# The first x tile as two transfers, and a query product ahead of the second tile's transposes

## The chip, the cores and the metric

The kernel runs on one core of a Trainium2 chip. The core has five engines that run side by side and synchronise by semaphores: PE (TensorE, matrix products; its weight loads are shown apart as PEld), DVE (VectorE), ACT (ScalarE), POOL (GpSimd) and SP (SyncE, here used to issue DMA transfers). ACT and POOL issue DMA transfers too. The metric is the device time of one execution in microseconds, the median of several executions.

## The reference

A gated mix of two branches over x, which has 2048 tokens of 640 features, in bf16. Cut to what matters:

```
x = A_x                                            # 1 x 2048 x 640
g = sigmoid((x * gate_w).sum(-1))
# branch A: linear attention, 32 heads of 20
q, k, v = split(x @ wqkv)
phi(t) = where(t > 0, t + 1, exp(t)) + 1e-6
o = (phi(q) @ (phi(k).T @ v)) / (phi(q) . sum(phi(k)) + 1e-6)      # per head
a = o @ wo
# branch B: token-shift mixer and MLP
h  = gelu(layernorm(x) @ w1);  hs = shifted(h) @ w2;  x1 = x + hs
b  = x1 + gelu(layernorm(x1) @ w3) @ w4
out = g * a + (1 - g) * b
```

The change touches the very first step, the query product q = x @ wqkv[:, 0:640] for the first two tiles of tokens.

## The kernel before, in words

Tokens are handled in 16 tiles of 128. The 640 features are 5 slices of 128. A product x @ w for one tile sums over the 5 slices: for each slice the turned x (features on the partitions, tokens along the free axis; the buffer `xT`) is loaded into PE as weights and the matching 128 rows of w stream through. So before a tile's products, x must be turned. x tiles 0 and 1 are loaded as they are into `x_tok` and turned by PE (a product with the identity matrix `ident`, which POOL makes at the start), from where DVE copies the turned slices out of PSUM into `xT`. Tiles 2 and 3 come straight from memory by a transposing DMA, and the later tiles are turned by DMA out of `x_tok`.

The kernel's own planner records every operation. Helpers work out which semaphores each operation has to wait for, so many operations carry a helper's line number: `tr_group` (L642) for turns by PE, `copy` (L696) for DVE's copies, `dma` (L286 and L282) for transfers, `warmup` (L913) and `stream` (L953). Work on PE is a list of named items. In each stream of items the order is fixed; between streams the planner picks by modelled times. In the opening only one stream, "A", has ready items, so the order there is what the code writes: `("warm",)`, `("tx", 0)`, `("warm", 1)`, `("q", 2)`, `("k", 2)` (L976 to L980).

- `("warm",)` issues products of constants that nobody reads: 6 of 512 columns and 3 of 128 (`WARM` = 3456 columns). They run while the first transfers are on their way.
- `("tx", 0)` is `t_x(0)` (L806): it turns slice 0 of tile 0 into one PSUM bank, then slices 1 to 4 into another, with one DVE copy behind each: 128 columns, and 512 columns.
- `("warm", 1)` is one more product of 128 columns (`WARM2` = 128).
- `("q", 2)` is `q_three` (L960): the query products of tiles 0, 1 and 2, of 512 columns each, in an order written out by hand as pairs (tile, slice). A pair with None stands for other work: (1, None) turns tile 1 (five turns, and DVE copies of slice 0, slices 1 and 2, and slices 3 and 4), and (2, None) is a small product for the gate weights (L611 in the profile, by `mm_group`).
- `("k", 2)` is the same for the keys of three tiles.

Transfers are issued at the start in this order. SP: x tile 0, x tile 1, wq slice 2, the transposed load of tile 2, then wk slices 0, 2 and 4 (the first of these waits until x tile 0 has landed), the transposed load of tile 3, and x tiles 4, 2, 3 and 5. ACT: wq slices 0, 1, 3 and 4, then wk slices 1 and 3. Each engine issues its transfers one after another; each issue takes it some 0.4 us, and a transposing one more than 1 us.

Of the kernel before, what the change touches and what calls it, by code (L numbers as in the profile page):

```python
# [11 lines left out]
D = 640  # L12
# [5 lines left out]
KD = D // 128  # L18
# [399 lines left out]
def _build(nc, A_x, A_wqkv, A_wo, B_w1, B_w2, B_w3, B_w4, gate_w, out, dbg=None, stop=None):  # L418
# [46 lines left out]
    def psb(b, n0, n1):  # L465
        return ps[:, b, :].bitcast(BF16)[:, n0:n1]
# [7 lines left out]
    x_tok = pa.alloc("x_tok", [128, NT, D], BF16)  # L474
# [46 lines left out]
    def bank():  # L521
        best = None
        for k_ in range(nbanks[0]):
            b = (bank_rr[0] + k_) % nbanks[0]
            if b in bank_pend or b in bank_hold:
                continue
            lk = sch.locks.get(b)
            tfree = 0.0 if lk is None else sch.ev_time.get((lk[1].sem, lk[1].val), 1e18)
            if best is None or tfree < best[0]:
                best = (tfree, b)  # L530
        bank_rr[0] = best[1] + 1
        bank_pend.add(best[1])
        return best[1]
# [50 lines left out]
    def dve(fn, reads, writes, cost=None):  # L584
        if cost is None:
            n = nfree(writes[0])
            cost = 65.0 + n / 0.96
        return sch.op("dve", fn, reads, writes, cost=cost)
# [7 lines left out]
    def pe(fn, reads, writes, cost=500.0, after=None):  # L596
        for w_ in writes:
            sp_, rl = sch.rects(w_)
            if sp_ == "ps":
                for (_p0, _p1, lo, hi) in rl:  # L600
                    for b in range(lo // PS_BANK, (hi - 1) // PS_BANK + 1):
                        bank_pend.discard(b)
        return sch.op("pe", fn, reads, writes, cost=cost, after=after)
# [32 lines left out]
    def tr_group(b, srcs):  # L636
        outs = [psb(b, 128 * i, 128 * (i + 1)) for i in range(len(srcs))]

        def fn(e, outs=outs, srcs=srcs):
            ins = None  # L640
            for o, s_ in zip(outs, srcs):
                ins = e.transpose(o, s_, ident[:])  # L642
            return ins
        return pe(fn, list(srcs) + [ident[:]], [psb(b, 0, 128 * len(srcs))], cost=len(srcs) * 56.0)
# [47 lines left out]
    def copy(engf, out_ap, in_ap):  # L692
        cost = None
        if engf is dve and in_ap.dtype == BF16 and out_ap.dtype == BF16:
            cost = 65.0 + nfree(out_ap) / 1.92
        return engf(lambda e: e.tensor_copy(out_ap, in_ap), [in_ap], [out_ap], cost=cost)  # L696
# [5 lines left out]
    x2 = A_x[0]  # L702

    def dma_in(out_ap, in_ap, key, **kw):
        return sch.dma("sp", out_ap, in_ap, key, **kw)

    def load_x(t):
        dma_in(x_tok[:, t, :], x2[128 * t:128 * (t + 1), :], "x%d" % t)

    def load_wq(k, queue):  # L710
        sch.dma(queue, wq[:, k, 0:512], A_wqkv[128 * k:128 * (k + 1), 0:512], "wq%d" % k)
# [7 lines left out]

    gwr = xn[:, 1, 0:128]  # L720
    dve(lambda e: e.memset(gwr, 0.0), [], [gwr])
    load_x(0)
    load_wq(0, "act")
    load_x(1)
    load_wq(1, "act")
# [74 lines left out]
        assert tags.get((buf, sl)) == what, ("stale ring slot", buf, sl, what, tags.get((buf, sl)))  # L800

    IT = _Items()
    WARM = 3456
    WARM2 = 128

    def t_x(t):  # L806
        for k0, k1 in ((0, 1), (1, KD)):
            b = bank()
            tr_group(b, [x_tok[:, t, 128 * k:128 * (k + 1)] for k in range(k0, k1)])
            for j0, j1 in {(1, 1): ((1, 3), (3, KD))}.get((t, k0), ((k0, k1),)):  # L810
                copy(dve, xT[:, j0:j1, 128 * t:128 * (t + 1)], psb(b, 128 * (j0 - k0), 128 * (j1 - k0)).rearrange("p (k c) -> p k c", k=j1 - j0))
# [6 lines left out]
    def phi(b, dst, after_exp=None, n=D):  # L818
        se = slot("E", 3)
        src = psf[:, 512 * b:512 * b + n]  # L820
        er = Er[:, se, 0:n]
        activation(er, src, ACTF.Exp)
        if after_exp is not None:
            after_exp()
        ts(dve, er, er, 1.0, EPS_PHI, ALU.min, ALU.add)
        return stt(dst, src, 1.0 + EPS_PHI, er, ALU.add, ALU.max)
# [75 lines left out]
        tag_chk("xn", sx, (which, t))  # L902
        sch.dma("sp", xnT[:, :, 128 * t:128 * (t + 1)], xn[:, sx, :], "trn%d" % slot("trn", 4), transpose=True)

    def warmup(cols, cyc):
        b = bank()
        one = nc.const_aps.tensor(1.0, [128, 512], BF16)
        steps = [512] * (cols // 512) + [128] * (cols % 512 // 128)

        def fn(e):  # L910
            ins = None
            for n in steps:
                ins = e.matmul(ps[:, b, 0:n], one[:, 0:128], one[:, 0:n], start=True, stop=True)  # L913
            return ins
        pe(fn, [], [ps[:, b, :]], cost=cols * cyc)
# [19 lines left out]
    def stream(order, w, n2, done):  # L935
        bs = {}
        for t in sorted({t for t, k in order if k is not None}):
            if not n2 and t == 1:
                bank_rr[0] += 1
            bs[t] = pair() if n2 else bank()  # L940
            bank_hold.update((bs[t], bs[t] + 1) if n2 else (bs[t],))
        for t, k in order:
            if k is None:
                if t is None:
                    warmup(256, 0.42)
                else:
                    t_gate() if t == 2 else t_x(t)
                continue
            b = bs[t]
            l = xT[:, k, 128 * t:128 * (t + 1)]  # L950

            def fn(e, l=l, b=b, k=k):
                ins = e.matmul(ps[:, b, 0:512], l, w[:, k, 0:512], start=(k == 0), stop=(k == KD - 1))  # L953
                return ins if not n2 else mm_kept(e, ps[:, b + 1, 0:n2], l, w[:, k, 512:512 + n2], k == 0, k == KD - 1)
            pe(fn, [l, w[:, k, 0:512 + n2]], [ps[:, b, 0:512]] + ([ps[:, b + 1, 0:n2]] if n2 else []), cost=272.0 if n2 else 216.0)
            if k == KD - 1:
                bank_hold.difference_update((b, b + 1) if n2 else (b,))
                done(t, b)

    def q_three():  # L960
        order = [(0, 0), (1, None), (0, 1), (1, 0), (1, 1), (0, 2), (2, None), (1, 2), (0, 3), (1, 3), (0, 4), (1, 4),
                 (2, 0), (2, 1), (2, 2), (2, 3), (2, 4)]
        stream(order, wq, 0, lambda t, b: phi(b, pq_tok[:, t + 1, 0:512], n=512))

# [8 lines left out]
    def addA(name, dur, fn, deps=()):  # L973
        IT.add("A", name, dur, fn, deps)

    addA(("warm",), 0.0, lambda: warmup(WARM, 0.834))  # L976
    addA(("tx", 0), 0.28, lambda: t_x(0))
    addA(("warm", 1), 0.0, lambda: warmup(WARM2, 0.42))
    addA(("q", 2), 3.24, q_three)
    addA(("k", 2), 4.08, k_three)  # L980
    for i in range(3, NT + 2):
# [489 lines left out]
    order = IT.run(sch, hook)  # L1471
# [6 lines left out]
def bass_gated_mix__linear_attn_block__mixer_s_mlp__prompt_kernel(  # L1478
    nc, A_x, A_wqkv, A_wo, B_x, B_w1, B_w2, B_w3, B_w4, gate_w, out
):  # L1480
    assert tuple(A_x.shape) == (1, S, D) and tuple(out.shape) == (1, S, D)
    assert tuple(A_wqkv.shape) == (D, 3 * D) and tuple(A_wo.shape) == (D, D)
    assert tuple(B_w1.shape) == (D, D) and tuple(B_w2.shape) == (D, D)
    assert tuple(B_w3.shape) == (D, F) and tuple(B_w4.shape) == (F, D) and tuple(gate_w.shape) == (D,)
    _build(nc, A_x, A_wqkv, A_wo, B_w1, B_w2, B_w3, B_w4, gate_w, out)
# [28 lines left out]
```

## Time and profile before

| | |
|---|---|
| time, median of 3 runs | 258.38 us (258.35 to 258.62) |
| the profiled execution's own time | 258.38 us |
| its span, first to last instruction | 257.1 us |
| PE busy | 252.7 us, 98% |
| DVE, ACT, POOL busy | 144.8, 107.0, 91.1 us |
| share of PE in the chain that ended last | 95% |
| HBM read, written | 12.04 MB, 2.62 MB |

Times in the profile count from the first instruction of the span. Matmuls are pipelined and the end that is recorded for one is modelled, so two neighbours overlap in the records: the distance from start to start is what a product costs in a row of them. "Chain" is the chain of work that ended last, followed back from the last instruction. An entry "A <- B" among the waits means that A's engine stood idle until B was done; "issue" stands for time in which nothing that the profile shows was waited for. Landing times of transfers are given from their issue.

### The profile page before, as it was taken

What the parts mean: (1) busy time and instruction counts of PE and PEld (TensorE: products, weight loads), DVE (VectorE), ACT (ScalarE), POOL (GpSimd) and SP (SyncE); (2) the same over time, 40 slices, a digit from 0 to 9 for tenths busy, and PEclk for the clock granted to TensorE, in tenths of its full rate; (3) what the DMA queues carried; (4) which work ended last, traced back from release to release, by engine and by line L of the source; (5) the groups of instructions that cost most, each with busy time, mean ns of one, the idle gap of its engine ahead of it and who ended that gap; (6) DMA issues with size and microseconds to landing.
All of it is one profiled execution on the core that took longest, in us unless ns stands there. A gap on an engine that the chain in (4) does not pass through costs nothing.

```text
span 257.1 us, 3575 instructions
## 1 busy us (share of the span) xinstructions
PE 252.7 (98%) x1387; PEld 111.0 (43%) x1237; DVE 144.8 (56%) x286; ACT 107.0 (42%) x219; POOL 91.1 (35%) x146
## 2 busy tenths in 40 slices
PE   8999999999999999999999999999999999999996
PEld 4333333344454343334444444444444444444444
DVE  2488888899953995589999604759100033200033
ACT  1496676651366848656655600003520100253000
POOL 5011499977862152858908002123000021300000
PEclk9999999999999999999999999999999999999999
DMA  7975689535743599362565400032100012200003
GB/s 194 291 150 123 187 162 234 182 78 126 122 93 70 100 357 373 75 102 60 121 105 127 103 10 20 9 119 51 28 0 0 20 32 93 102 1 3 0 20 102
DMA packets 58577, 26.65 MB, mean 104 GB/s; under 512 B 49900, under 2 KB 57149, under 8 KB 58560
## 3 DMA queue, kind: packets, MB, share of 16 engines
q1 hardware_dynamic: 56304, 22.17, 36.1%
q0 software_dynamic: 1168, 3.28, 5.1%
q10 hardware_dynamic: 1088, 0.98, 1.2%
q8 instruction: 10, 0.16, 0.3%
q14 instruction: 7, 0.06, 0.1%
HBM read 12.04 MB, written 2.62 MB: 57 GB/s over the span
## 4 chain that ended last, share of the span: by engine, by line
PE 95%; DVE 2%; ACT 1%; issue 1%
PE ps L611 35%; PE ps L1251 30%; PE ps L630 12%; PE ps L840 7%; PE ps L619 4%; PE ps L953 2%; PE ps L913 1%; PE ps L1297 1%; PE ps L1157 1%; ACT Er L687 1%; DVE Er L653 1%; DVE pk_tok L670 1%; ACT junk L686 1%; PE ps L642 0%; PE ps L1040 0%
## 5 line engine op out<-in xcount | busy, mean ns | idle before, releaser
L611 PE MATMUL ps<-xnT,w 128*128 128x512 bf16 x352 | 79.9, 379 | 0.5 <-issue 0.2
L670 DVE SCALAR_TENSOR_TENSOR x_tok<-ps,stg,abx 128x512 bf16<-128x512 f32 (+2 forms) x17 | 12.2, 719 | 78.6 <-PE ps L1251 78.5
L687 ACT ACTIVATE h2T<-ps 128x512 bf16<-128x512 f32 x52 | 30.7, 597 | 59.8 <-PE ps L611 59.8
L611 PEld LDWEIGHTS ps<-xnT,w 128*128 128x128 bf16 x360 | 34.7, 98 | 41.5 <-issue 2.1
L1251 PE MATMUL ps<-w,h2T 128*128 128x512 bf16 (+2 forms) x218 | 45.9, 366 | 0.3 <-issue 0.2
L653 POOL TENSOR_SCALAR xn<-x_tok,st 128x640 bf16<-128x640 bf16 x32 | 34.9, 1098 | 26.3 <-DMA xnT<-xn 25.7
L653 POOL TENSOR_SCALAR abx<-x_tok,stg 128x640 f32<-128x640 bf16 (+1 forms) x16 | 15.0, 944 | 70.8 <-DVE x_tok L670 70.8
L1251 PEld LDWEIGHTS ps<-w,h2T 128*128 128x128 bf16 x221 | 21.1, 98 | 24.1 <-issue 0.3
L687 ACT ACTIVATE Er<-ps 128x512 bf16<-128x512 f32 (+1 forms) x36 | 23.0, 651 | 14.0 <-PE ps L619 10.7
L686 ACT ACTIVATE junk<-x_tok 128x640 bf16<-128x640 bf16 x32 | 23.6, 738 | 3.9 <-DVE x_tok L668 3.7
L687 ACT ACTIVATE hsT<-ps 128x512 bf16<-128x512 f32 (+1 forms) x32 | 19.0, 593 | 13.5 <-PE ps L611 13.1
L630 PE MATMUL ps<-w,hsT 128*128 128x512 bf16 x76 | 22.3, 379 | 0.0
L668 DVE SCALAR_TENSOR_TENSOR x_tok<-ps,x_tok 128x640 bf16<-128x640 f32 x16 | 13.1, 821 | 10.8 <-PE ps L619 10.2
L1251 PE MATMUL ps<-M_sb,pqnT 128*128 128x512 bf16 (+2 forms) x83 | 18.7, 366 | 0.1
L630 PE MATMUL ps<-wkg,xT 128*128 128x512 bf16 x63 | 18.7, 379 | 0.0
L840 PE MATMUL ps<-pk_tok,x_tok 128*128 128x512 bf16 x79 | 17.7, 379 | 0.1
L619 PE MATMUL ps<-wkg,xT 128*128 128x130 bf16 x80 | 17.6, 220 | 0.2
L619 PE MATMUL ps<-w,hsT 128*128 128x128 bf16 x80 | 17.5, 219 | 0.2
L1186 DVE TENSOR_TENSOR pq_tok<-pq_tok,dnr 128x300 bf16<-128x300 bf16 (+1 forms) x48 | 17.1, 412 | 0.6
L653 DVE TENSOR_SCALAR Er<-Er 128x512 bf16<-128x512 bf16 (+1 forms) x36 | 12.3, 340 | 8.1 <-ACT Er L687 7.4
L611 PE MATMUL ps<-wq,xT 128*128 128x512 bf16 x64 | 15.9, 379 | 0.1
L661 DVE TENSOR_TENSOR qprod<-qprod,pk_tok 128x640 f32<-128x640 f32 x13 | 15.7, 1209 | 0.4
(90 smaller groups left out, 252.4 us busy)
## 6 DMA issues: line engine op xcount, KB each, us to landing
w<-in_B_w_dram SPq DMA_DIRECT2D x1, 2160.0 KB, 8.1
w<-in_B_w_dram SPq DMA_DIRECT2D x1, 2080.0 KB, 13.2
out_dram<-x_tok SPq DMA_DIRECT2D x3, 640.0 KB, 3.1
w<-in_B_w_dram POOLq DMA_DIRECT2D x8, 160.0 KB, 3.9
x_tok<-in_A_x_dram SPq DMA_DIRECT2D x6, 160.0 KB, 3.8
x_tok<-in_A_x_dram SPq DMA_DIRECT2D x1, 960.0 KB, 5.5
wv<-in_A_wqkv_dram POOLq DMA_DIRECT2D x1, 800.0 KB, 5.3
x_tok<-in_A_x_dram SPq DMA_DIRECT2D x1, 640.0 KB, 4.3
```

The lines of the kernel that those rows point to most:

```text
L611: ins = e.matmul(out_ap, l, r, start=(i == 0), stop=(i == n - 1))
L619: return e.add_instruction(mybir.InstMatmult(name=nc.get_next_instruction_name(), engine=e.engine, ins=[e.lower_ap(r), ll], outs=[e.lower_ ...
L630: e.matmul(outs[0], l, r, start=st, stop=sp, skip_group_check=True)
L653: return engf(lambda e: e.tensor_scalar(out_ap, in_ap, s1, s2, op0, op1), rd, [out_ap], cost=cost)
L661: return engf(lambda e: e.tensor_tensor(out_ap, a, b_, op), [a, b_], [out_ap], cost=cost)
L668: return dve(lambda e: e.scalar_tensor_tensor(out_ap, in0, scalar, in1, op0, op1, accum_out=accum), rd, [out_ap, accum], cost=cost + 70.0)
L670: return dve(lambda e: e.scalar_tensor_tensor(out_ap, in0, scalar, in1, op0, op1), rd, [out_ap], cost=cost)
L686: return act(lambda e: e.activation(out_ap, in_ap, func, bias=bias, scale=scale, accum_out=accum), rd, wr, cost=cost)
L687: return act(lambda e: e.activation(out_ap, in_ap, func, bias=bias, scale=scale), rd, wr, cost=cost)
L840: ins = e.matmul(o, l, r, start=(t0 + q_ == 0), stop=(t0 + q_ == NT - 1))
L1186: dve(lambda e, o=o, i0=i0, i1=i1: e.tensor_tensor(o, i0, i1, ALU.mult), [i0, dnr[:, 1, sd, :]], [o], cost=cost)
L1251: ins = e.matmul(o, l, r, start=first and i == 0, stop=last and i == len(prs) - 1, skip_group_check=True)
```

## The change

Three edits belong together.

1. x tile 0 is loaded by two transfers of SP's queue instead of one: first its columns 0 to 127 (slice 0, 32 KB), with a semaphore of its own, then columns 128 to 639 (slices 1 to 4, 128 KB) with the semaphore that the whole tile had. SP has one more transfer to issue, ahead of all others.
2. The opening on PE becomes: 5 warm-up products of 512 columns; the turn of slice 0, which waits for the first transfer; 4 warm-up products of 128 columns; the turns of slices 1 to 4, which wait for the second transfer; then the query products. The 3 narrow warm-up products ahead of the turns and the one behind them are gone.
3. In `q_three`, the pair (0, 1), tile 0 with slice 1, moves ahead of (1, None), the turns of tile 1.

The orders of instructions on DVE, ACT and POOL are as before, and so is PE's behind the pair (1, 1). On PE, the opening reads so (before to the left):

```
6 x warm-up, 512 columns                5 x warm-up, 512 columns
3 x warm-up, 128 columns                turn tile 0, slice 0    (waits for transfer 1, identity)
turn tile 0, slices 0 to 4              4 x warm-up, 128 columns
1 x warm-up, 128 columns                turn tile 0, slices 1-4 (first waits for transfer 2)
query (0,0)                             query (0,0)
turn tile 1, slices 0 to 4              query (0,1)             (waits for wq slice 1 and DVE's copy)
query (0,1)                             turn tile 1, slices 0 to 4
query (1,0), (1,1), (0,2), gate         query (1,0), (1,1), (0,2), gate
```

```diff
-    load_x(0)
+    dma_in(x_tok[:, 0, 0:128], x2[0:128, 0:128], "x0a")
+    dma_in(x_tok[:, 0, 128:D], x2[0:128, 128:D], "x0")
...
-    WARM = 3456
-    WARM2 = 128
+    WARM = 2560
+    WARM2 = 512
 
-    def t_x(t):
-        for k0, k1 in ((0, 1), (1, KD)):
+    def t_x(t, parts=((0, 1), (1, KD))):
+        for k0, k1 in parts:
...
-    def warmup(cols, cyc):
+    def warmup(cols, cyc, wide=512):
...
-        steps = [512] * (cols // 512) + [128] * (cols % 512 // 128)
+        steps = [wide] * (cols // wide) + [128] * (cols % wide // 128)
...
-        order = [(0, 0), (1, None), (0, 1), (1, 0), (1, 1), (0, 2), (2, None), (1, 2), (0, 3), (1, 3), (0, 4), (1, 4),
+        order = [(0, 0), (0, 1), (1, None), (1, 0), (1, 1), (0, 2), (2, None), (1, 2), (0, 3), (1, 3), (0, 4), (1, 4),
...
-    addA(("tx", 0), 0.28, lambda: t_x(0))
-    addA(("warm", 1), 0.0, lambda: warmup(WARM2, 0.42))
+    addA(("tx", 0), 0.06, lambda: t_x(0, ((0, 1),)))
+    addA(("warm", 1), 0.0, lambda: warmup(WARM2, 0.834, 128))
+    addA(("tx", 1), 0.22, lambda: t_x(0, ((1, KD),)))
```

## The prediction

> **What bounds the kernel now.** I read the page's first and fourth parts, then the waits of PE past the opening, then the chain of waits and the timeline of the first 9 us, where every edit lies. The page:
>
> ```profile
> span 257.1 us, 3575 instructions
> PE 252.7 (98%) x1387; PEld 111.0 (43%) x1237; DVE 144.8 (56%) x286; ACT 107.0 (42%) x219; POOL 91.1 (35%) x146
> PE 95%; DVE 2%; ACT 1%; issue 1%
> ```
>
> PE is the bound. The list of who waited for whom, for PE from 6.5 us to the end, holds two entries:
>
> ```profile
> PE ps L611 <- issue: 0.2, 1, 0.2
> PE ps L1251 <- issue: 0.2, 1, 0.2
> ```
>
> So in 250 us PE waits for no transfer and for no engine longer than it takes to hide. Whatever the opening gains or loses is handed on to the end one for one. The chain of the opening (start, length, what):
>
> ```profile
> 0.83 3.04 PE ps L913 x9
> 3.87 0.53 PE ps L642 x5
> 4.40 0.11 PE ps L913
> 4.51 0.43 PE ps L953
> 4.94 0.53 PE ps L642 x5
> 5.47 1.17 PE ps L953 x4
> 6.64 0.01 PE ps L611
> ```
>
> L913 is the warm-up, L642 the turns of x tiles 0 and 1, L953 the query products, L611 the small gate product. There is no gap. A 512-column product costs 0.43 us, a 128-column one 0.11, five turns 0.53. The timeline gives the same by starts; my yardstick is the start of the gate product:
>
> ```profile
> 0.83 3.04 PE L913 MATMUL ps<-const-bfloat16-1.0 128*128 128x512 bf16 x9 [0.83 <-PEq L1499]
> 3.68 0.72 PE L642 MATMUL ps<-ident,x_tok 128*128 128x128 bf16 x5
> 4.73 0.74 PE L642 MATMUL ps<-ident,x_tok 128*128 128x128 bf16 x5
> 5.26 1.37 PE L953 MATMUL ps<-wq,xT 128*128 128x512 bf16 x4
> 6.47 0.17 PE L611 MATMUL ps<-ident,xn 128*128 128x5 bf16 x1
> 6.50 2.32 PE L953 MATMUL ps<-wq,xT 128*128 128x512 bf16 x10
> 8.66 0.38 PE L953 MATMUL ps<-wkg,xT 128*128 128x512 bf16 x1
> ```
>
> Ten query products start between 6.50 and 8.66, 0.216 us each: half of the 0.43 before. The four from 5.26 take 1.21 us to the gate product; with slow time s, s/0.43 + (1.21 - s)/0.216 = 4, so s = 0.69 and PE's pace doubles at about 5.95 us, 5.1 us after its first product (the page's granted clock reads full throughout, so only the spacing shows it). The gate product starts at 6.47; the change is worth what it moves that start.
>
> **The change part by part.** DVE's copies out of PSUM are what the new order meets:
>
> ```profile
> 4.01 0.23 DVE L696 COPY xT<-ps 128x128 bf16<-128x128 bf16 x1 [3.02 <-PE ps L642]
> 4.44 0.42 DVE L696 COPY xT<-ps 128x512 bf16<-128x512 bf16 x1 [0.20 <-PE ps L642]
> 5.08 0.23 DVE L696 COPY xT<-ps 128x128 bf16<-128x128 bf16 x1 [0.22 <-PE ps L642]
> 5.51 0.49 DVE L696 COPY xT<-ps 128x256 bf16<-128x256 bf16 x2 [0.20 <-PE ps L642]
> ```
> ```profile
> 5.51 0.29 DVE L696 COPY xT<-ps 128x256 bf16<-128x256 bf16 x1 [0.20 <-PE ps L642]
> ```
> ```profile
> 5.85 0.29 PEld L953 LDWEIGHTS ps<-wq,xT 128*128 128x128 bf16 x2 [0.39 <-DVE xT L696]
> ```
>
> A copy starts 0.35 us after the start of a lone turn (4.73 to 5.08), or 0.04 after the recorded end of a group (4.40 to 4.44); PE's weight load follows the copy's end by 0.05 (5.80 to 5.85). The transfers, by the DMA view's issues (KB, us from issue to landing), for x tile 0, x tile 1, and slices 0 and 1 of wq:
>
> ```profile
> x_tok<-in_A_x_dram SPq DMA_DIRECT2D x1, 160.0 KB, 2.8
> wq<-in_A_wqkv_dram ACTq DMA_DIRECT2D x1, 128.0 KB, 3.0
> ```
> ```profile
> x_tok<-in_A_x_dram SPq DMA_DIRECT2D x1, 160.0 KB, 3.0
> ```
> ```profile
> wq<-in_A_wqkv_dram ACTq DMA_DIRECT2D x1, 128.0 KB, 3.3
> ```
>
> and the timeline's rows of the issues, and of POOL's identity matrix, which every turn needs:
>
> ```profile
> 0.79 0.87 SPq L286 DMA_DIRECT2D x_tok<-in_A_x_dram  x2
> 1.71 0.43 SPq L286 DMA_DIRECT2D wq<-in_A_wqkv_dram  x1
> 2.19 1.30 SPq L282 DMA_TRANSPOSE xT<-in_A_x_dram  x1
> 3.65 1.40 SPq L286 DMA_DIRECT2D wkg<-in_A_wqkv_dram  x3
> ...
> 0.80 1.86 ACTq L286 DMA_DIRECT2D wq<-in_A_wqkv_dram  x4
> ...
> 2.41 0.29 POOL L699 TENSOR_SCALAR_AFFINE_SELECT ident<-ones_c 128x128 bf16<-128x128 bf16 x1
> ```
>
> x tile 0 lands at 0.79 + 2.8 = 3.6 and is turned at 3.68; x tile 1, SP's second issue at 0.79 + 0.87 - 0.40 = 1.26, lands at 4.3; wq slice 1, ACT's second of four at about 1.24, at 4.5. The identity is ready at 2.70.
>
> *Warm-up.* Five wide products instead of six, and no three narrow ones: PE is free at 0.83 + 3.04 - 0.20 (the recorded tail by which a group's length exceeds its spacing, 0.72 against 0.53) - 0.32 - 0.43 = 2.92. The lone narrow product between turns and query goes (-0.11); four narrow ones (0.43) come behind slice 0's turn.
>
> *Slice 0 (32 KB, issued at 0.79).* It lands no later than the whole tile did (3.6), and earlier than 2.92 is of no use. I take 3.0. Turn and narrow products then end near 3.55, and any landing up to 3.4 is hidden behind the next item.
>
> *Slices 1 to 4 (128 KB).* They are now the second issue of SP's queue, at 1.26. From below: PE's own work ends at 2.92 + 0.11 + 0.43 = 3.46, so landing earlier is of no use. From above: 4.3, what x tile 1 shows for that place in the queue with more bytes ahead. By bytes they are the rest of what landed at 3.6; by time from issue (2.8 to 3.3) they land at 4.1 to 4.5. I take 3.95, midway between the two x tiles' landings, and the four turns at 4.03 (0.08 behind, as before). The Trainium skill's page "DMA: Bandwidth & Descriptors", section "Anatomy of one DMA — SWDGE (gpsimd) path", fits a transfer as 2.0 us plus its bytes over 436 GB/s, which as an estimate lands them at 3.56; with that the working below ends at 6.74 and the time at 258.65. The trace doesn't agree: wq slice 0, of the same size and alone on its queue, took 3.0 us and not 2.3, and the page states the fit for the software queue; so I keep the row.
>
> *The sequence from 4.03.* Four turns to 4.46; their recorded end is 4.03 + 0.72 - 0.11 = 4.64, so the 512-wide copy runs 4.68 to 5.10. Query (0,0) runs 4.46 to 4.89. Query (0,1), which needs slice 1 out of that copy, cannot start before 5.15: 0.26 idle. Before the change tile 1's turns (0.53) stood exactly there. (0,1) runs to 5.58. Tile 1's turns start at 5.58 and, with the pace doubling at 5.95, end at 6.04. Copy of slice 0 from 5.93 to 6.16, so (1,0) starts at 6.21: 0.17 idle, where before query (0,1) was the cover. Recorded end of the turns about 6.20, first paired copy 6.24 to 6.53, so (1,1), after (1,0) ended at 6.43, starts at 6.58: 0.15 idle. (0,2) from 6.80, gate product at 7.01.
>
> The sum, 7.01 - 6.47 = +0.54 us, split: turns start 0.35 later (4.03 against 3.68), idle 0.58, narrow product gone -0.11, and -0.28 because half a microsecond of this work now falls behind 5.95 and runs at double pace. At landing 3.45 (turns at 3.46) the same working gives a gate product at 6.56, +0.09; at 4.3 (turns at 4.38) 7.21, +0.74.
>
> *SP's queue.* One more issue puts everything behind it 0.43 to 0.45 us later: x tile 1 lands near 4.75 (needed at 5.58), wq slice 2 near 6.0 (needed at 6.80). The first wk issue, which waits for x tile 0's last part and for the transpose ahead of it, moves from 3.65 to 4.0. Its rows, with that of the transposed load of tile 2 and of wq slice 2:
>
> ```profile
> wkg<-in_A_wqkv_dram SPq DMA_DIRECT2D x1, 160.0 KB, 4.0
> ```
> ```profile
> xT<-in_A_x_dram SPq DMA_TRANSPOSE x1, 4.6
> ```
> ```profile
> wq<-in_A_wqkv_dram SPq DMA_DIRECT2D x1, 128.0 KB, 3.8
> ```
>
> wk slice 0 lands at 8.0 instead of 7.65 and is needed at 8.66 + 0.54; tile 2 at 7.25 instead of 6.8, needed five products after 6.50, 7.58 + 0.54. Nothing is added to the sum; if these covers were gone it would be at most the 0.45. Later loads find PE without any wait, above. ACT, DVE and POOL keep their orders.
>
> The profiled execution took 258.38 us (span 257.1 and 1.28 around it), the median of the runs. 258.38 + 0.54 = 258.92, +0.21%.
>
> **The rivals.**
>
> *The pace doubles later (slower).* The row "0.83 3.04" and all behind it are gapless for the 5.1 us that the doubling took. After the change there is a gap before 4.03 (about 0.5), and 0.26 before 5.15. If 5.1 us of gapless work are needed from the last long gap, doubling comes at 9.13. All work to the gate product is then slow: (1,0) 6.21 to 6.64, (1,1) 6.70, (0,2) 7.13, gate 7.55; from there 1.58 us of slow pace lose 0.79. Sum 7.55 - 6.47 + 0.79 = 1.87: 260.25. If only the busy time has to add up to 5.1, doubling comes some 0.8 later and the time is 259.2. For it: the one doubling seen followed gapless work. Against: nothing in this trace shows a gap that hurt. The Trainium skill's page "TensorE: Matmul & The Clock Gate", section "What's actually happening", has the gate judged in free-running windows of 3.4 us by how busy PE was. 5.1 us after the first product agrees with one half-filled window and one full one; were the full one now judged too idle, the step would come a window later, at about 9.36, and the time would be 260.4 as an estimate.
>
> *The second part lands early (not slower).* It decides at 3.93: below it the loss is under 0.2%, and at 3.45 the time is 258.47, because the 0.22 earlier start and the dropped narrow product pay most of the DVE waits. For it: tile 0 whole was there at 3.6. Against: issue is 0.47 later, and the first transfers took 2.8 to 3.3 us.
>
> *The change doesn't do what it says (slower).* Slice 0 lands no earlier than the whole tile, 3.6; turn and four narrow products, now in its way, end at 3.68 + 0.54 = 4.22: gate product at about 7.13, 259.04. Against: a fifth of the bytes.
>
> **How the numbers follow.** The sum with landing 3.75 to 4.3: 0.56, of which 0.33 beyond 0.2% slower, 0.23 within. Doubling later: 0.22, all slower. Early landing: 0.10, within 0.2%. Slice 0 late: 0.06, slower. A gain that I see no row for: 0.06. So faster 0.06, within 0.33, slower 0.61; 0.2% (0.52 us) is about what a measurement of this kernel can tell from no change. The likeliest case's own range is 258.6 to 259.15. Cutting the gain at the low end and the top of the late doubling at the other leaves 258.4 to 260.3.
>
> **What the profile after would show.** Right: the four turns near 4.0 with PE idle before them; (0,1)'s weights released by DVE's 512-wide copy with some 0.3 us idle; smaller such waits for (1,0) and (1,1); the gate product near 7.0; everything after it shifted alike, with no new wait. Wrong: turns of slices 1 to 4 at 3.5 (early landing), query products still 0.43 apart behind 6.5 us (doubling later), slice 0's turn at 3.7, or a wait for a transfer on PE behind 6.5 us.

## The result and the profile after

The changed kernel takes 260.06 us (median of 13 executions, 258.95 to 261.49) against 258.32 us before (13 executions, 257.87 to 258.78): a ratio of 1.0069, 95% interval 1.0056 to 1.0082. It is slower, by 1.74 us between the medians; the forecast was +0.54. The executions spread over 2.5 us, those of before over 0.9; in two of the 13 (260.96 and 261.49 us) the granted clock was 0.993 on average, in the others 1.0. The profiled execution took 260.06 us too, with a span of 258.8.

PE's timeline of the changed kernel:

```profile
0.83 2.29 PE L914 MATMUL ps<-const-bfloat16-1.0 128*128 128x512 bf16 x5 [0.83 <-PEq L1501]
2.97 0.29 PE L642 MATMUL ps<-ident,x_tok 128*128 128x128 bf16 x1
3.05 0.63 PE L914 MATMUL ps<-const-bfloat16-1.0 128*128 128x128 bf16 x4
3.80 0.61 PE L642 MATMUL ps<-ident,x_tok 128*128 128x128 bf16 x4
4.20 1.33 PE L954 MATMUL ps<-wq,xT 128*128 128x512 bf16 x2
6.26 0.45 PE L642 MATMUL ps<-ident,x_tok 128*128 128x128 bf16 x5 [0.73 <-DMA x_tok<-in_A_x_dram]
6.81 0.90 PE L954 MATMUL ps<-wq,xT 128*128 128x512 bf16 x3
7.54 0.17 PE L611 MATMUL ps<-ident,xn 128*128 128x5 bf16 x1
7.57 1.24 PE L954 MATMUL ps<-wq,xT 128*128 128x512 bf16 x5
9.31 1.25 PE L954 MATMUL ps<-wq,xT 128*128 128x512 bf16 x5 [0.50 <-DMA xT<-in_A_x_dram]
10.40 0.38 PE L954 MATMUL ps<-wkg,xT 128*128 128x512 bf16 x1
```

Two waits for transfers stand where there was none: tile 1's turns wait for x tile 1 until 6.26, and the query products of tile 2 wait for its transposed load until 9.31. (An idle time here is counted from the recorded end of the product before, 0.2 us after PE could have started the next.) The gate product starts 1.07 us later than before (7.54 against 6.47), the first key product 1.74 later (10.40 against 8.66), and the two profiled executions differ by 1.68: behind 10.4 us nothing more is lost. The weight loads of the opening show DVE's part of it:

```profile
3.79 0.35 PEld L642 LDWEIGHTS ps<-ident,x_tok 128*128 128x128 bf16 x4 [0.38 <-DMA x_tok<-in_A_x_dram]
4.92 0.10 PEld L954 LDWEIGHTS ps<-wq,xT 128*128 128x128 bf16 x1 [0.67 <-DVE xT L696]
6.26 0.28 PEld L642 LDWEIGHTS ps<-ident,x_tok 128*128 128x128 bf16 x5 [1.23 <-DMA x_tok<-in_A_x_dram]
6.81 0.10 PEld L954 LDWEIGHTS ps<-wq,xT 128*128 128x128 bf16 x1 [0.27 <-DVE xT L696]
7.10 0.12 PEld L954 LDWEIGHTS ps<-wq,xT 128*128 128x128 bf16 x2 [0.20 <-DVE xT L696]
```

Landings, from the DMA view: first and second part of x tile 0, x tile 1, the transposed load of tile 2 (issued at 0.79, 1.26, 1.71 and 2.66):

```profile
x_tok<-in_A_x_dram SPq DMA_DIRECT2D x1, 32.0 KB, 2.1
...
x_tok<-in_A_x_dram SPq DMA_DIRECT2D x1, 128.0 KB, 2.5
...
x_tok<-in_A_x_dram SPq DMA_DIRECT2D x1, 160.0 KB, 4.5
...
xT<-in_A_x_dram SPq DMA_TRANSPOSE x1, 6.6
```

The first part lands at 2.9, the second at 3.75, but x tile 1 at 6.2 instead of 4.3 and tile 2 at 9.3 instead of 6.8. One more issue of 0.45 us comes with landings 1.9 and 2.5 us later. The two windows of 1 us that show it, with the rate of all transfers in the last column (columns: window, length, PE busy and count, granted clock, DMA share, GB/s), before:

```profile
3.25:4.25 1.00, 1.00 (x10) 1.00 1.06 349
5.25:6.25 1.00, 1.00 (x6) 1.00 1.24 164
```

and after:

```profile
3.25:4.25 1.00, 0.88 (x10) 1.00 1.02 256
6.25:7.25 1.00, 0.89 (x7) 1.00 0.96 114
```

The engines that move data are about as busy (DMA shares 0.96 to 1.24) but move less: a first dip from 3.25 us that before didn't have, and a second, which both have and which comes later after the change. ACT's issues point at one difference. Its wk loads wait for wq slice 0, which lands at 0.80 + 2.3 = 3.1 (before at 3.8; the only transfer issued ahead of it is now 32 KB and not 160), so they are issued at 3.12 instead of 3.82:

```profile
wq<-in_A_wqkv_dram ACTq DMA_DIRECT2D x1, 128.0 KB, 2.3
...
3.12 0.89 ACTq L286 DMA_DIRECT2D wkg<-in_A_wqkv_dram  x2
```

### The profile page after: what moved, and what is told of

The parts are those of the page before. It is cut to its first block, busy times and chain, and to the rows that moved or that the text cites. A ratio compares the mean times of both kernels' runs of the same rounds, so it can differ in the third digit from the quotient of the medians.

```text
span 258.8 us, 3574 instructions
## 1 busy us (share of the span) xinstructions
PE 252.9 (98%) x1386; PEld 110.2 (43%) x1236; DVE 143.9 (56%) x286; ACT 107.0 (41%) x219; POOL 89.9 (35%) x146
## 4 chain that ended last, share of the span: by engine, by line
PE 90%; DVE 3%; DMA 3%; ACT 1%; issue 1%; SPq 1%
PE ps L611 34%; PE ps L1253 30%; PE ps L630 12%; PE ps L841 7%; PE ps L619 4%; DMA xT<-in_A_x_dram 3%; PE ps L954 1%; PE ps L1299 1%; PE ps L1159 1%; ACT Er L687 1%; DVE Er L653 1%; SPq L286 1%; DVE pk_tok L670 1%; ACT junk L686 1%; DVE x_tok L668 0%
## 5 line engine op out<-in xcount | busy, mean ns | idle before, releaser
L668 DVE SCALAR_TENSOR_TENSOR x_tok<-ps,x_tok 128x640 bf16<-128x640 f32 x16 | 13.1, 820 | 10.7 <-PE ps L619 10.1
L661 DVE TENSOR_TENSOR qprod<-qprod,pk_tok 128x640 f32<-128x640 f32 x13 | 15.1, 1165 | 0.4
```

The source lines that it names most:

```text
L661: return engf(lambda e: e.tensor_tensor(out_ap, a, b_, op), [a, b_], [out_ap], cost=cost)
L668: return dve(lambda e: e.scalar_tensor_tensor(out_ap, in0, scalar, in1, op0, op1, accum_out=accum), rd, [out_ap, accum], cost=cost + 70.0)
```

## The experiments

Twelve kernels, four theories in turn. Ratios are against the kernel before on the same chip, with 95% intervals.

**1. The split alone.** The kernel before with x tile 0 in two transfers; PE's order is untouched.

```diff
-    load_x(0)
+    dma_in(x_tok[:, 0, 0:128], x2[0:128, 0:128], "x0a")
+    dma_in(x_tok[:, 0, 128:D], x2[0:128, 128:D], "x0")
```

> The kernel before with x tile 0 in two transfers, PE's order left as it was. Theory A (the extra or earlier transfers upset the later ones: x tile 1 and the transposed load of tile 2 land 1 to 2 us late, as in the changed kernel's profile): x tile 1 lands after 5.5 us, PE waits for it, 259.3 to 260.3, and executions spread by over 1.5 us. Theory B (the loss is in PE's new order alone, by the DVE waits of the forecast): within 0.2 us of before, 258.3 to 258.5, landings at most 0.5 us later.

259.83 us, 1.0076 (1.0053 to 1.0099): all of the change's loss, without its order. Turns at 3.67 as before, then:

```profile
6.20 0.45 PE L642 MATMUL ps<-ident,x_tok 128*128 128x128 bf16 x5 [1.51 <-DMA x_tok<-in_A_x_dram]
```

Theory A holds; theory B falls.

**2. The order alone.**

```diff
-        order = [(0, 0), (1, None), (0, 1), (1, 0), ...
+        order = [(0, 0), (0, 1), (1, None), (1, 0), ...
```

> The kernel before with query (0,1) ahead of tile 1's turns, nothing else. By the forecast's working from turns at 3.68: (0,1) waits for DVE's 512-wide copy until 4.93, (1,0) starts at 5.99, (1,1) at 6.48, gate product at 6.91: +0.44, 258.75, with a spread like before's. Theory A expects the same here, and that this is only a part of the 1.7 us. Theory B expects the whole loss here, 259.5 or more.

258.53 us, 1.0013 (1.0002 to 1.0024): +0.34 us by the ratio, 0.45 between the medians, where 0.44 was worked out. The three DVE waits are there, as the weight loads of (0,1), (1,0) and (1,1) show:

```profile
4.70 0.10 PEld L953 LDWEIGHTS ps<-wq,xT 128*128 128x128 bf16 x1 [0.33 <-DVE xT L696]
5.46 0.10 PEld L953 LDWEIGHTS ps<-wq,xT 128*128 128x128 bf16 x1 [0.27 <-DVE xT L696]
5.75 0.11 PEld L953 LDWEIGHTS ps<-wq,xT 128*128 128x128 bf16 x2 [0.20 <-DVE xT L696]
```

Their price rests on the times of all executions and not on this profile, which is of the quickest one (258.09): its pace had doubled by 3.73, and its gate product starts at 6.20, earlier than before the change. The waits don't add visibly to the 0.76% of the split: in the changed kernel PE waits for x tile 1 behind (0,1) anyway, and from tile 1's turns to the gate product the changed kernel and kernel 1 both take 1.28 us.

**3 and 4. When ACT's wk loads start.** In 3, the changed kernel with both wk loads of ACT waiting for x tile 0's second part; in 4, the kernel before with them waiting for nothing.

```diff
-                deps=[sch.dma_last["x0" if queue == "sp" else "wq0"]])
+                deps=[sch.dma_last["x0"]])                                  # 3
+                deps=[sch.dma_last["x0"]] if queue == "sp" else [])         # 4
```

> The changed kernel, but ACT's two wk loads wait for the second part of x tile 0 (landed 3.75) instead of wq slice 0 (landed 3.1). Theory A1 (wq slice 0 lands 0.7 us earlier and so releases 320 KB of wk loads into the transfers of x tile 1, wq and tile 2): x tile 1 lands by 4.8, the transposed load by 7.4, 258.6 to 259.0 and a spread under 1 us. Theory A2 (the later place on SP's queue alone is to blame): 259.7 to 260.3, spread as in the changed kernel.

> The kernel before, but ACT's two wk loads wait for nothing and are issued right behind wq slice 4, at about 2.7 and 3.1 us. Theory A1: x tile 1 or the transposed load of tile 2 lands 1 us or more later, PE waits, 259.2 to 260.5 with a wide spread. Theory A2: no more than 0.3 us from before.

Kernel 3: 259.91 us, 1.0061 (1.0038 to 1.0084). The transposed load of tile 2 lands 4.7 us after its issue, at 7.3 instead of 9.3, as theory A1 has it; x tile 1 still lands 4.1 after its issue, at 5.8, as A2 has it. The time doesn't decide between the two, because the six executions fall in two groups, 258.97 to 259.40 and 260.42 to 260.70, and the profiled one is the slowest. In it the query products are still 0.43 us apart until about 9.7 us:

```profile
5.89 0.71 PE L642 MATMUL ps<-ident,x_tok 128*128 128x128 bf16 x5 [0.37 <-DMA x_tok<-in_A_x_dram]
...
7.89 3.27 PE L954 MATMUL ps<-wq,xT 128*128 128x512 bf16 x10
11.00 0.38 PE L954 MATMUL ps<-wkg,xT 128*128 128x512 bf16 x1
```

From tile 1's turns (5.89) to the first key product (11.00) it took 5.11 us. With the pace doubled, the changed kernel took 1.28 to the gate product, and the kernel before 2.19 from there. By these figures, as an estimate, some 1.6 of its 260.70 us are the pace, and without that it would have taken 259.1, as the quicker three did. Kernel 4: 259.61 us, 1.0058 (1.0045 to 1.0072): x tile 1 lands at 4.3 as ever, but tile 2's load takes 6.7 us from 2.19 and PE waits for it:

```profile
8.95 1.25 PE L953 MATMUL ps<-wq,xT 128*128 128x512 bf16 x5 [1.25 <-DMA xT<-in_A_x_dram]
```

So two things are at work. The earlier wk loads make tile 2 late, by about 2 us; something else makes x tile 1 late. (They aren't the only thing that can delay tile 2: in kernels 7 and 8 below it lands at 8.1, with ACT's wk loads issued from 4.2 on.)

**5 and 6. The place on the queue, or the 256-byte pieces.** In 5, the kernel before (one transfer for x tile 0) with wq slice 2 issued second and x tile 1 third. In 6, the changed kernel with a first part of 256 columns.

```diff
     load_wq(1, "act")        # 5: x tile 1 behind wq slice 2
     load_wq(2, "sp")
+    load_x(1)
```
```diff
+    dma_in(x_tok[:, 0, 0:256], x2[0:128, 0:256], "x0a")     # 6
+    dma_in(x_tok[:, 0, 256:D], x2[0:128, 256:D], "x0")
```

> The kernel before, whole x tile 0, but SP issues wq slice 2 second and x tile 1 third (at 1.71 us, as in the changed kernel). Theory P (the place: whatever SP issues third meets a stretch from about 3.3 us in which the transfer engines stall): x tile 1 lands at 5.4 or later, PE waits for it, 259.0 to 260. Theory S (the split itself, with the 256-byte pieces of its first part, upsets the engines): x tile 1 lands near 4.9 with its 16 parts within 0.8 us, PE waits 0.2, 258.2 to 258.6.

> The changed kernel with the first part 256 columns wide (pieces of 512 bytes instead of 256), the rest 384. Theory P: x tile 1 still lands at 5.6 or later, 259.6 to 260.3. Theory S: x tile 1 by 5.0, 258.7 to 259.1.

Kernel 5: 259.18 us, 1.0046 (1.0026 to 1.0066). Without any split x tile 1 takes 4.4 us from 1.71 and lands at 6.1:

```profile
6.14 0.45 PE L642 MATMUL ps<-ident,x_tok 128*128 128x128 bf16 x5 [1.20 <-DMA x_tok<-in_A_x_dram]
```

Kernel 6: 260.00 us, 1.0066 (1.0040 to 1.0092), x tile 1 at 1.71 + 4.3 = 6.0. The narrow pieces aren't it; the place on the queue is enough. And kernel 5 has no first dip (332 GB/s from 3.25), so x tile 1 can be this late without one.

**7 and 8. The second part on ACT's queue.** The changed kernel with slices 1 to 4 as ACT's first transfer; 8 has the old order of query products as well.

```diff
-    dma_in(x_tok[:, 0, 128:D], x2[0:128, 128:D], "x0")
+    sch.dma("act", x_tok[:, 0, 128:D], x2[0:128, 128:D], "x0")
```

> The changed kernel, but slices 1 to 4 of x tile 0 come as ACT's first transfer, so that x tile 1 is SP's second again, and wq slices 0, 1, 3, 4 each go one place down on ACT. Theory P: x tile 1 lands by 4.5; wq slice 1, now third on ACT, lands near 5.2 and (0,1) waits for it; 258.6 to 259.2. Theory S: x tile 1 lands at 5.4 or later, 259.5 to 260.3.

> As the kernel with the rest of x tile 0 on ACT's queue, and query (0,1) behind tile 1's turns again, as before the change. Theory P: x tile 1 by 4.5, the turns cover DVE's copy and wq slice 1's landing, 258.0 to 258.5, level with before or a little under it. Theory S: 259.3 to 260.2.

259.43 us, 1.0058 (1.0031 to 1.0086), and 259.23 us, 1.0045 (1.0029 to 1.0061). In both x tile 1, second again, lands by 4.1, and wq slice 1, now third on ACT, is what lands late (6.4 and 6.1 us), later than the 5.2 that I had put down for kernel 7. PE waits for it instead; the waits of kernel 8's opening:

```profile
PE ps L954 <- DMA wq<-in_A_wqkv_dram: 1.0, 2, 0.8
```

Theory P was right on which transfer is late, and too hopeful on the time: both kernels came out between the two theories' ranges, 0.1 us under theory S's. The profile of kernel 7 is of its slowest execution (261.52; the others go down to 258.65). In it PE waited 1.6 us for wq slice 1, until 6.5, and some 1.7 us later the granted clock (the number behind PE's count) fell to half:

```profile
8.25:9.25 1.00, 1.00 (x4) 0.50 1.06 389
```

In the five windows of 1 us from 7.25 it reads 0.95, 0.50, 0.50, 0.50 and 0.85. As an estimate from these, 1.7 us of this execution are lost to the clock, beside the wait itself.

**9 and 10. What slows the third place.** In 9, tile 2's transposed load goes behind SP's three wk loads; in 10, POOL's transfer of the gate weights goes behind POOL's set-up work.

```diff
-    sch.dma("sp", xT[:, :, 256:384], x2[256:384, :], "trx2", transpose=True)
     ...
     load_wk(4, "sp")
+    sch.dma("sp", xT[:, :, 256:384], x2[256:384, :], "trx2", transpose=True)    # 9
```
```diff
     memset(pool, hsT[:, :, S:S + 4], 0.0)
+    sch.dma("pool", xn[0:KD, 1, 0:128], gate_w.rearrange("(k p) -> k p", p=128), "gw")    # 10
```

> The changed kernel with tile 2's transposed load behind SP's three wk loads, just ahead of tile 3's. Theory X (issuing and running the transposed load stalls the transfers under way, so whatever is third lands late): x tile 1 lands by 5.0, PE does not wait for it, and the time lost is that of tile 2, which now lands near 9 to 9.5 and is needed at 8.1: 259.4 to 260. Theory G (POOL's gate transfer does it): x tile 1 still lands at 5.8 or later, 260 to 261.

> The changed kernel with POOL's transfer of the gate weights issued behind POOL's set-up work, near 4 us instead of 1.3. Theory G: x tile 1 lands by 5.0, and the time falls to 258.8 to 259.4. Theory X: x tile 1 at 5.8 or later, and 259.8 to 260.4 as in the changed kernel. In both, the gate product may wait for its data until about 7.

Kernel 9: 260.29 us, 1.0081 (1.0066 to 1.0095), because tile 2 is now what is late (PE waits for it until 9.54, and 0.6 us for slices 1 to 4 of tile 0, until 4.33). But x tile 1 lands 3.5 us after its issue, at 5.2, and the second dip is gone:

```profile
3.25:4.25 1.00, 0.49 (x5) 1.00 0.93 261
4.25:5.25 1.00, 0.65 (x5) 1.00 1.08 376
5.25:6.25 1.00, 0.87 (x7) 1.00 1.01 333
```

So the running transposed load is the second dip and about 1 us of x tile 1's lateness. The first dip, at 3.25, stays. Kernel 10: 260.66 us without the profiled execution of 264.39 (260.87 with it), 1.0109 (1.0076 to 1.0142). The profiled one had a granted clock of 0.50 from 9.25 to 12.25 us, so I use only the start of it. x tile 1 takes 3.9 us, landing at 5.6, and the rate from 3.25 is 247 GB/s, while no packet of POOL's queue moves between 3.2 and 7.4: the gate transfer makes no dip. Issued at 3.3 it lands only at 9.7, and PE waits 2.6 us for it.

**11 and 12. Another split, and none of PE's data third.** In 11, the kernel before with x tile 0 split by rows, whole 1280-byte pieces. In 12, the changed kernel with x tile 1 second on ACT, wq slice 1 on POOL's queue, and kernel 3's edit.

```diff
-    load_x(0)
+    dma_in(x_tok[0:64, 0, :], x2[0:64, :], "x0a")          # 11
+    dma_in(x_tok[64:128, 0, :], x2[64:128, :], "x0")
```
```diff
-    load_x(1)
-    load_wq(1, "act")
+    sch.dma("act", x_tok[:, 1, :], x2[128:256, :], "x1")   # 12
+    load_wq(1, "pool")
```

> The kernel before with x tile 0 in two transfers by rows (tokens 0 to 63, then 64 to 127, whole 1280-byte pieces), PE's order as before. Theory N (one more transfer ahead is enough: x tile 1 goes third, ACT's wk loads come earlier): x tile 1 lands at 5.6 or later with packets of 0.5 us or more among those that start at 3.3 to 4.1, 259.4 to 260.3, like the split by columns. Theory C (narrow column pieces of the same rows are what stalls x tile 1's packets): no such packets before 4.1, x tile 1 by 5.3, 258.6 to 259.3.

> The changed kernel, with x tile 1 as ACT's second transfer, wq slice 1 on POOL's queue ahead of the gate weights, and ACT's wk loads waiting for x tile 0's second part, so that nothing that PE needs before 6.5 us is third on SP or ACT. If late transfers are what the changed kernel lost beyond the forecast's sum, x tile 1 lands by 4.7, PE's opening is the forecast's (DVE waits of 0.3, 0.2 and 0.1 us, gate product near 6.8), and the time is 258.6 to 259.2. If late transfers come with the split wherever they stand, x tile 1 or wq slice 1 lands after 5.3 and the time is 259.5 or more.

Kernel 11: 261.04 us, 1.0112 (1.0097 to 1.0127), the deepest dip but one:

```profile
3.25:4.25 1.00, 0.62 (x4) 1.00 0.85 197
4.25:5.25 1.00, 0.00 (x0) 1.00 0.91 256
```

x tile 1 lands at 2.06 + 4.2 = 6.3. Tile 0's own second part, 80 KB, takes 4.0 us from 1.44, and that is what PE waits for first: the turns start at 5.57 and not at 3.67 (the view names no releaser):

```profile
5.57 0.69 PE L642 MATMUL ps<-ident,x_tok 128*128 128x128 bf16 x5 [1.70 <-issue]
```

Of the two theories N holds, as one more transfer in the opening is enough, by rows as by columns; but the time is above its range, because of this wait, which neither theory had, and of products that are 0.43 us apart until about 10.1. Kernel 12: 260.39 us, 1.0077 (1.0051 to 1.0103). x tile 1 lands at 4.2, but wq slice 1 takes 4.1 us on POOL's queue, and PE waits for it until 5.6. POOL, busy with that issue, makes the identity later too (slice 0's turn waits for POOL until 3.40), and products are 0.43 us apart until about 8.9. The late slice bears out the second theory of the expectation only in part, as POOL's queue was new to it; whether the split could pay with all data on time stays untried. No kernel here beats the one before.

## Why the prediction was right or wrong

The sign was right, and the measured 260.06 lies within the range (258.4 to 260.3); the size, +0.54, was a third of the +1.74. That the range held is luck in part. The sum's own case went to 259.15, and the range reached 260.3 only for the later doubling, while the profiled execution lost its time to two late transfers that the forecast put at nothing. One of its signs of being wrong is there: a wait for a transfer on PE behind 6.5 us (tile 2, at 9.31). By its steps:

- *What the opening loses is handed on.* Right: 1.74 at the first key product, 1.68 at the end.
- *Warm-up, slice 0, slices 1 to 4.* Nearly right. The first turn stood at 2.97 (2.92 to 3.0 in the working), the four turns at 3.80 (4.03): the second part landed 2.5 us after its issue, where 2.7 was taken (3.95 - 1.26). This term was 0.23 too dear. The estimate from the Trainium skill's page "DMA: Bandwidth & Descriptors", section "Anatomy of one DMA — SWDGE (gpsimd) path", put that landing at 3.56, 0.2 too early.
- *The DVE waits.* Right in place and size. (0,1) started 1.12 us behind the turns in the working (4.03 to 5.15) and 1.12 in the trace (3.80 to 4.92). Alone, the order cost 0.34 us, 0.05 to 0.62 by its interval, for 0.44.
- *The doubled pace.* Put at 5.95, it had happened by 6.26 in this execution, where five turns take 0.45 us and not 0.74.
- *SP's queue.* This is the step that failed: "One more issue puts everything behind it 0.43 to 0.45 us later", x tile 1 "near 4.75", tile 2 "at 7.25", "Nothing is added to the sum". They landed at 6.2 and 9.3, and PE waited 0.9 and 0.7 us. I moved each landing by the delay of its issue, with the time from issue to landing held fixed. It wasn't fixed. Third on its queue, x tile 1 took 4.4 to 4.5 us for 3.0, with the split or without it (kernel 5), and 3.5 when the transposed load ran later (kernel 9). And I looked at one queue only: the smaller first transfer let wq slice 0 land 0.7 us sooner, which released ACT's wk loads into tile 2's transposed load (kernels 3 and 4).

Of the rivals, early landing (below 3.93) came true, but its gain was lost in the wait for x tile 1; slice 0 was not late. The later doubling did not happen in the profiled execution of the changed kernel, but it does occur: in the profiled executions of kernels 3, 8, 11 and 12 products are 0.43 us apart until about 9.7, 10.1, 10.1 and 8.9. In all four PE had waited in the opening. In the three profiles without a wait for a transfer before 6 us (before, 2 and 4) the pace had doubled by 5.95 at the latest; but so it had, by 6.5, in the other seven with such a wait. That fits the rival, that idle time can put the doubling off, without proving it. Kernel 8, in which PE waited 0.4 us near 4 and 1.0 us near 5.3, shows it so:

```profile
6.28 1.86 PE L954 MATMUL ps<-wq,xT 128*128 128x512 bf16 x4 [0.80 <-DMA wq<-in_A_wqkv_dram]
7.94 0.21 PE L611 MATMUL ps<-ident,xn 128*128 128x5 bf16 x1
8.01 3.35 PE L954 MATMUL ps<-wq,xT 128*128 128x512 bf16 x10
```

What share of the changed kernel's spread is due to this, what to a clock that falls again (kernel 7) and what to the landings, which one profile per kernel can't tell, stays open. Open too is what makes the first dip. The rate from 3.25 to 4.25 us is 332 to 372 GB/s in the four kernels with x tile 0 whole (before, 2, 4, 5) and 180 to 309 in the ten with it split: neither the gate transfer, nor the transposed load, nor the size of the pieces makes it.

## What to carry to other kernels

Before adding or moving a transfer in an opening that is full of transfers, look up what each later one took from issue to landing at the place that it will have, not at the place that it had. Here x tile 1 took 3.0 us in the second place and 4.5 in the third. The row of the third place stood in the profile before, 3.8 us for the 128 KB of wq slice 2; it would have put x tile 1 at 1.71 + 3.8 = 5.5 and not at 4.75, with next to nothing left to the 5.58 at which the forecast needed it. That is still short of the 6.2 measured, but it would have called for a term in the sum. Then follow every queue, not only the one that is edited, because a transfer that lands sooner releases its waiters sooner, and these may collide with something that PE needs first. A cover that is taken away (turns over a DVE copy) has about the price that the timeline gives, but if a longer wait stands at the same place, it isn't added. And look at the pace and the granted clock of the profiled execution before its time is put down to what PE waited for.

## What the runs showed of the hardware

- A transposed load takes the rate of all transfers down while it runs: 164 GB/s against 315 in the microsecond ahead of it in the kernel before, and 333 at the same time in kernel 9, which ran it later. The load of tile 2 took 6.1 to 7.2 us in the six kernels in which ACT's first wk load of 160 KB was issued by 3.4 us (changed, 1, 4, 6, 10, 11), 4.4 to 5.0 in five with later ones (before, 2, 3, 5, 12), and 5.9 in kernels 7 and 8, with later ones too.
- The granted clock can fall to half again early in an execution: in kernel 7's profile, by its five windows from 7.25, for some 3.4 us, after PE had waited 1.6 us. The wait alone isn't shown to be the cause, as kernel 1's profile, with 1.5 us of waiting until 6.2, reads 1.00 throughout.
- The time of PE's doubling differs from execution to execution of nearly the same opening: near 5.95 us before, but by 3.73 us in kernel 2, where the five turns already take 0.45 us:

```profile
3.73 0.45 PE L642 MATMUL ps<-ident,x_tok 128*128 128x128 bf16 x5
```

So 5.1 us of gapless work are not what it needs, as one of the rivals supposed. The Trainium skill's page "TensorE: Matmul & The Clock Gate", section "What's actually happening", has free-running windows of 3.4 us. Kernel 7's 3.4 us at half the granted clock agree with that length. The doublings, as an inference, don't speak against it: 2.9 us after the first product in kernel 2, and in kernel 8, with 1.4 us of waits, more than 7 us after it, fit windows that have to be mostly, but not wholly, busy.
